# PV of all units in plain float32 on 64 columns a head, and a third raw tile for each of the mixture's weights

## The chip, the cores and the metric

The kernel runs on one core of a Trainium2 chip. The metric is the device time of one execution in microseconds (us). Engines in the profile: PE is TensorE (PEld its weight loads), DVE is VectorE, ACT is ScalarE, POOL is GpSimd, SP issues DMA transfers.

## The reference

Inputs are q, k and v of shape (4, 8, 576, 64): 4 batches, 8 heads, 576 positions, 64 elements a head. Everything is float32.

```
scores = (q @ k.T) / 8; position i sees position j where i // 64 >= j // 64, others get -1e9
attn   = softmax of scores over the last axis (maximum taken off, 1e-9 added to the sum)
x      = attn @ v, heads side by side: 2304 tokens x 512
p      = domain_probs / (sum over the 4 experts + 1e-9)
out    = sum over e of p[:, e] * (relu(x @ w1[e]) @ w2[e])   # w1[e] 512 x 1024, w2[e] 1024 x 512
```

## The kernel before, in words

**Two precisions.** A float32 product is made in one of two ways. Split: both operands are cut into a high part and a low part in float32r (a cast, then a subtraction), and the products of the parts are added up in PSUM. Plain: TensorE multiplies float32 as it is.

**The mixture** works on five blocks of tokens (BLOCKS): a first one of 256 (the first 64 positions of the four batches) and four of 512 (positions 64 to 575 of one batch each). A block has 32 chunks (4 experts, 8 slices of 128 hidden units). A chunk is mm1 (12 matmuls of the split form, L1035), the relu split into hh and hl, and mm2 (per 128 tokens 3 matmuls, L1080) into four accumulators. For each chunk, 256 KB of w1 and of w2 are loaded to a raw tile (w1r, w2r, two of each), cast to w1h or w2h and subtracted to w1l or w2l (four of each). A raw tile comes free when its subtraction is done.

**The attention.** The first block's attention is done at the start by itself. The rest is 16 units: one pair of heads of one batch, 512 queries against 576 keys. The scores are kept transposed, keys on partitions, queries on columns, in five pieces of 512, 448, 320, 192 and 64 columns (pieces_of); C = 1536 is their sum. The last piece, of 64 keys, has both heads on one half of the partitions each. Units of batch 0 (plain, ph == 1) run during the mixture's first block; the four units of batch b run during the mixture's block of batch b - 1. The code spreads a unit over threads: k_thread, q_thread, v_thread (loads and splits), s_thread (scores into two PSUM banks, att), e_thread (out of PSUM into the tile S, and a running maximum in cm), m_thread (maximum over keys by GpSimd, subtraction, exponential), pv_flow (product with V, normalization, and x split into xh and xl).

**What differs by unit before the change.** In the four plain units, by_piece subtracts and exponentiates piece by piece over both heads, sum_up adds the pieces into sa, and pv_flow makes, in one stretch on TensorE, the product with V in float32 with each head's 64 columns on its own half of the PSUM partitions (L777), and then the sums over keys by a matmul with ones. V comes straight into a tile VN, whose middle 64 columns hold ones. In the twelve other units, exp_head takes the exponential of a whole head (L715), casts 1472 columns to PH and subtracts to PL; V is loaded to vr and split into VS; for each head the product is a chain of nine steps in one bank: four pieces of PH against [Vh, Vl], the 64-column piece in plain float32 against VJ, four pieces of PL (L809). The bank's two halves are then added (a copy to rc and an addition to xs). The sums are added in place in S and reduced over partitions by GpSimd (L733).

**What sets the order.** Flow is a planner that runs when the program is built: each thread yields operations, with the engine or engines that may do it, a cost in ns, what it reads and the buffers it uses. The planner keeps a clock for each engine and emits the operation that can start first by its estimate (ties by priority). A thread that wants a buffer (take) waits until one is given back. So each engine's queue has one order written down beforehand, and an engine stands where the next instruction's inputs are late, whatever else is ready behind. `late` tells the planner to assume a further delay (LAG / 2 = 750 ns for the product with V).

Of the kernel before, what the change touches and what calls it, by code (L numbers as in the profile page):

```python
# [9 lines left out]
F32R = mybir.dt.float32r  # L10
# [7 lines left out]
PEO = 13.5  # L18


NARROW = 64
# [185 lines left out]
def kernel(  # L207
# [50 lines left out]
    wide_of = [[x[2] for x in pieces_of(j[1], j[2])[0] if x[2] > NARROW] for j in every]  # L258
    MAXE = max(sum(x) for x in wide_of)
    MAXT = max(len(x) for x in wide_of)  # L260
# [12 lines left out]
    bufs("w1r", 2, [P, KC, P])  # L273
    bufs("w2r", 2, [P, DM])
# [7 lines left out]
    bufs("vr", 1, [P, MAXT, 2, D])  # L282
# [5 lines left out]
    bufs("VS", 2, [P, MAXT, 4, D], F32R)  # L288
    bufs("VJ", 2, [P, 2, 3, D])
# [4 lines left out]
    bufs("PL", 2, [P, MAXE], F32R)  # L294
    bufs("PH", 2, [P, MAXE], F32R)
    bufs("cm", 1, [P, 2 * MAXW])
    bufs("mx", 1, [P, 2 * MAXW])
    bufs("sa", 1, [P, 2 * MAXW])
    bufs("xs", 1, [P, MAXW])
# [27 lines left out]
    def late(o, by):  # L327


        o.lag = by  # L330
        return o
# [52 lines left out]
    def unit(u, ua, us, ju, pu, ph, job, dst, c):  # L384
# [5 lines left out]
        wide, narrow = [x for x in pcs if x[2] > NARROW and not plain], [x for x in pcs if x[2] <= NARROW or plain]  # L390
        ce = sum(x[2] for x in wide)
# [67 lines left out]
        def v_thread():  # L459
            yield ("until", lambda: now[0] >= gate[u])  # L460
            vals, jv, got = [], [], []
            n = len(wide)
            VS = None
            VJ = yield (fl.take("VN", u) if plain else fl.take("VJ", us))
            if n:
                vr = yield fl.take("vr", us)
                VS = yield fl.take("VS", us)
                for h in range(2):
                    vals.append((yield dma(vr.tile[:, :n, h, :], v[b, h0 + h, :P * n].rearrange("(t p) d -> p t d", p=P),
                                           n * P * 256, u=[vr], prio=pr + 0.005)))  # L470
            keep = sorted(j for j, *_ in narrow if j is not None)
            for h in range(2):
                if plain:
                    jv.append((yield dma(VJ.tile[:, VJ.tile.shape[1] - 1, 2 * h, :], v[b, h0 + h, q1 - P:q1], P * 256,
                                         u=[VJ], prio=pr + 0.005)))
                elif odd:
                    jv.append((yield dma(VJ.tile[64 * h:64 * h + 64, VJ.tile.shape[1] - 1, 1, :], v[b, h0 + h, q1 - MASK_BLOCK:q1], 64 * 256,
                                         u=[VJ], prio=pr + 0.005)))
                if keep:
                    jv.append((yield dma(VJ.tile[:, :len(keep), 2 * h, :],  # L480
                                         v[b, h0 + h, P * keep[0]:P * keep[-1] + P].rearrange("(t p) d -> p t d", p=P),
                                         len(keep) * P * 256, u=[VJ], prio=pr + 0.005)))
            if n:
                vs = VS.tile[:, :n]
                a = yield a_copy(vs[:, :, 0:4:3, :], vr.tile[:, :n], n * 128, vals, [vr, VS], pr + 0.005)
                l = yield tt(BOTH, vs[:, :, 1:3, :], vr.tile[:, :n], vs[:, :, 0:4:3, :], SUB, n * 128, [a], [vr, VS],
                             pr + 0.005)
                got += [a, l]
                fl.give(vr)
            st["v"] = (VS, VJ, got, jv)  # L490

# [163 lines left out]
        def by_piece(Sb, Sv, mx, mv, m):  # L655
# [8 lines left out]
            def sum_up():  # L664
# [3 lines left out]
                for i, (_, a, w, c0) in enumerate(todo[1:]):  # L668
                    yield ("until", lambda: len(exps) > i + 1)
                    r = a - q0  # L670
                    if i == 0:
                        got.append((yield a_copy(av[:, :, :r], Sv[:, :, :r], 2 * r, exps[:1], [Sb, sa], pr)))
                    t = yield tt("dve", av[:, :, r:], av[:, :, r:] if i else Sv[:, :, r:W], Sv[:, :, c0:c0 + w], ADD, 2 * w,
                                 exps[i:i + 2] + got[1:], [Sb, sa], pr)
                    got = got[:1] + [t]
                for h in range(2):
                    st["P"][h] = (None, None, None, None, Sb, exps)
                st["sums"] = (sa, got)
# [8 lines left out]
        def m_thread():  # L687
# [13 lines left out]
            st["P"] = {}  # L701
            st["exp"] = []

            if plain:
                yield from by_piece(Sb, Sv, mx, mv, m)
                return
            subs = []
            for _, a, w, c0 in pcs:
                sv, mb = Sv[:, :, c0:c0 + w], mv[:, :, a - q0:W]
                subs.append((yield tt("dve", sv, sv, mb, SUB, 2 * w, [m] + st["evac"], [Sb, mx], pr)))  # L710
            fl.give(mx)

            def exp_head(h):
                PH = PL = a = l = None
                j = yield op("act", 0.833 * C + 95, lambda _: nc.scalar.activation(  # L715
                    Sv[:, h, :C], Sv[:, h, :C], AF.Exp, scale=scale), subs, [Sb], pr)
                if wide:
                    PH = yield fl.take("PH", pu + h)
                    PL = yield fl.take("PL", pu + h)
                    a = yield a_copy(PH.tile[:, :ce], Sv[:, h, :ce], ce, [j], [Sb, PH], pr)  # L720
                    l = yield tt("dve", PL.tile[:, :ce], Sv[:, h, :ce], PH.tile[:, :ce], SUB, ce, [j, a], [Sb, PH, PL], pr)
                st["P"][h] = (PH, PL, a, l, Sb, j)

            for h in range(2):
                yield from exp_head(h)

            got = [x for h in range(2) for x in st["P"][h][2:4] + st["P"][h][5:]]
            for _, a, w, c0 in pcs[1:]:
                acc = Sv[:, :, a - q0:W]
                got = [(yield tt("dve", acc, acc, Sv[:, :, c0:c0 + w], ADD, 2 * w, got, [Sb], pr))]  # L730
            st["sums"] = []
            for h in range(2):
                st["sums"].append((yield op("pool", 150 + 6.3 * W, lambda _, h=h: nc.gpsimd.partition_all_reduce(  # L733
                    Sv[:, h, W:2 * W], Sv[:, h, :W], P, RED.add), got, [Sb], pr)))
# [3 lines left out]
        fl.spawn(pv_flow(st, q0, dst, c, W, wide, narrow, C, plain, pr, bank_tag))  # L738
# [13 lines left out]

    def pv_flow(st, q0, dst, c, W, wide, narrow, C, plain, pr, bank_tag):
        yield ("until", lambda: "v" in st)
        VS, VJ, vv, jv = st["v"]
        xs = yield fl.take("xs")
        rc = yield fl.take("rc", st["ua"])
        parts, sums = [], []
        if plain:
            yield ("until", lambda: "sums" in st)  # L760
            sa, sv = st["sums"]
            PJ, pj = st["P"][1][4:]
            two = []
            for _ in range(2):
                two.append((yield fl.take("att", None, bank_tag)))

            def fn(_):

                for x, todo in zip(two, (narrow, [(None, None, W, 0)])):
                    for i, (j, _a, w, c0) in enumerate(todo):  # L770
                        for g in range(2):
                            if x is two[0]:
                                lhsT = VJ.tile[:, VJ.tile.shape[1] - 1 if j is None else j, 2 * g, :]
                                rhs = PJ.tile[:, g * C + c0:g * C + c0 + w]
                            else:
                                lhsT, rhs = VJ.tile[:, 0, 1, :], sa.tile[:, g * W:g * W + W]
                            nc.tensor.matmul(out=x.tile[64 * g:64 * g + 64, W - w:W], lhsT=lhsT, rhs=rhs,  # L777
                                             start=(i == 0), stop=(i == len(todo) - 1))

            m = yield op("pe", 450.0 + (C + W) / 0.6, fn, jv + pj + sv, [*two, VJ, PJ, sa], pr)  # L780
# [8 lines left out]
            sums.append((yield op([("act", 0.833 * W + 55), ("dve", 1.04 * W + 70)], 0, fn, [m], [two[1], rc], pr)))  # L789
            parts.append((yield a_copy(xs.tile[:, :W], two[0].tile[:, :W], W, [m], [two[0], xs], pr, True)))  # L790
            fl.give(*two)
        for h in range(0 if plain else 2):
            yield ("until", lambda: h in st.get("P", ()))
            PH, PL, a, l, PJ, pj = st["P"][h]
            pb = yield fl.take("att", None, bank_tag)
            ps = pb.tile
            todo = []
            for x, split, dep in ((PH, True, a), (PJ, False, pj), (PL, True, l)):
                for j, _a, w, c0 in wide if split else narrow:
                    if split:  # L800
                        lhsT, cost, dv, c1 = VS.tile[:, j, 2 * h:2 * h + 2, :], w / 2.4 + PEO, vv, c0
                    else:
# [410 lines left out]
```

## Time and profile before

| | us |
|---|---|
| median of 3 runs (lowest, highest) | 931.5 (931.19, 933.13) |
| the profiled execution | 932.45 |
| its span | 930.7 |
| PE, DVE, ACT, POOL busy | 915.3, 728.9, 438.2, 138.7 |
| granted TensorE clock | 0.999 |

The span is the time from the first to the last instruction in the trace. Matmuls are pipelined: the duration of one, as it is shown, overlaps the next, so the distance from start to start is what a matmul takes of TensorE's time.

### The profile page before, as it was taken

Reading aid. Unit: us, or ns where it says so; the run is one execution under the profiler, and the core shown is the slowest. Engines: PE = TensorE matmul, PEld = TensorE weight load, DVE = VectorE, ACT = ScalarE, POOL = GpSimd, SP = SyncE. Lnnn points to the kernel's source line nnn. Section 1 sums busy time; section 2 is a strip of 40 time slices with the busy share of each in tenths; the row PEclk is TensorE's granted clock in tenths of the full one; section 3 lists DMA queues with packets and bytes.
Section 4 is the critical chain, followed back from the end, with each engine's and each line's share of the span. In section 5 each row is a group of like instructions: output and inputs, shape, how many; then the busy total and the mean of one; then the engine's idle time right before and its main releaser. Section 6 shows DMA issues by size and latency. Waiting matters only on the chain.

```text
span 930.7 us, 12721 instructions
## 1 busy us (share of the span) xinstructions
PE 915.3 (98%) x4398; PEld 750.8 (81%) x4398; DVE 728.9 (78%) x1291; ACT 438.2 (47%) x774; POOL 138.7 (15%) x57
## 2 busy tenths in 40 slices
PE   8999999999999999999999999999999999999998
PEld 4677788888887888887888888888888888888886
DVE  7789999989897888878988888888988754445442
ACT  3577765655463454454454545464534322322220
POOL 1111101222103201212131202012121200000000
PEclk9999999999999999999999999999999999999999
DMA  9755466534532445351623545343423343333321
GB/s 166 181 163 165 136 154 189 116 115 93 145 85 80 113 140 137 108 135 46 149 72 100 128 121 154 104 105 113 116 90 90 92 148 102 92 100 94 100 57 45
DMA packets 236162, 107.97 MB, mean 116 GB/s; under 512 B 131393, under 2 KB 213313, under 8 KB 236097
## 3 DMA queue, kind: packets, MB, share of 16 engines
q1 hardware_dynamic: 232928, 106.38, 42.8%
q10 hardware_dynamic: 3168, 0.79, 0.5%
q8 instruction: 34, 0.56, 0.2%
q14 instruction: 32, 0.25, 0.1%
HBM read 102.40 MB, written 4.72 MB: 115 GB/s over the span
## 4 chain that ended last, share of the span: by engine, by line
PE 90%; DVE 4%; DMA 3%; ACT 1%; issue 1%; SPq 1%; DVEq 0%; ACTq 0%
PE acc L1080 40%; PE h L1035 40%; PE att L809 4%; PE att L539 2%; PE att L540 2%; DMA w1r<-in_moe_w_dram 1%; SPq L334 1%; PE acc L777 1%; PE att L777 1%; DVE w2l L347 1%; DMA S<-in_v_dram 1%; DVE cm L347 1%; PE att L527 1%; DVE w1l L347 0%; DMA w2r<-in_moe_w_dram 0%
## 5 line engine op out<-in xcount | busy, mean ns | idle before, releaser
L1035 PE MATMUL h<-xh,w1h 128*128 128x512 f32 (+1 forms) x640 | 237.9, 372 | 0.0
L1035 PE MATMUL h<-xh,w1l 128*128 128x512 f32 (+1 forms) x640 | 236.1, 369 | 1.6 <-DVE w1l L347 1.6
L1035 PE MATMUL h<-xl,w1h 128*128 128x512 f32 (+1 forms) x640 | 235.6, 368 | 0.1
L1080 PE MATMUL acc<-w2h,hh 128*128 128x512 f32 x576 | 227.0, 394 | 0.0
L1080 PE MATMUL acc<-w2h,hl 128*128 128x512 f32 x576 | 224.7, 390 | 1.0 <-DVE hl L1054 1.0
L1080 PE MATMUL acc<-w2l,hh 128*128 128x512 f32 x576 | 224.6, 390 | 0.0
L1052 ACT ACTIVATE hh<-h 128x512 fp32r<-128x512 f32 (+1 forms) x160 | 88.9, 556 | 184.6 <-PE h L1035 183.5
L347 DVE TENSOR_TENSOR w2l<-w2r,w2h 128x512 fp32r<-128x512 f32 x160 | 112.9, 706 | 56.2 <-ACT w2h L340 55.8
L340 ACT CAST w2h<-w2r 128x512 fp32r<-128x512 f32 x148 | 92.2, 623 | 136.1 <-PE acc L1080 132.0
L1035 PEld LDWEIGHTS h<-xh,w1l 128*128 128x128 f32 x640 | 120.4, 188 | 22.7 <-DVE w1l L347 2.4
L1035 PEld LDWEIGHTS h<-xh,w1h 128*128 128x128 f32 x640 | 120.5, 188 | 21.0 <-issue 1.2
L1035 PEld LDWEIGHTS h<-xl,w1h 128*128 128x128 f32 x640 | 120.6, 188 | 19.8 <-DVE xl L347 0.3
L1054 DVE SCALAR_TENSOR_TENSOR hl<-h,hh 128x512 fp32r<-128x512 f32 (+1 forms) x160 | 100.6, 629 | 35.9 <-ACT hh L1052 35.4
L1080 PEld LDWEIGHTS acc<-w2h,hl 128*128 128x128 f32 x576 | 108.1, 188 | 25.0 <-DVE hl L1054 1.9
L1080 PEld LDWEIGHTS acc<-w2h,hh 128*128 128x128 f32 x576 | 108.3, 188 | 23.9 <-issue 2.5
L347 DVE TENSOR_TENSOR w1l<-w1r,w1h 128x512 fp32r<-128x512 f32 x160 | 119.3, 745 | 8.2 <-ACT w1h L340 4.4
L1080 PEld LDWEIGHTS acc<-w2l,hh 128*128 128x128 f32 x576 | 108.3, 188 | 20.0
L733 POOL PARTITION_ALL_REDUCE S<-S x24 | 79.8, 3374 | 242.4 <-DVE S L347 223.9
L696 POOL PARTITION_ALL_REDUCE mx<-cm x16 | 54.4, 3398 | 355.8 <-DVE cm L347 270.3
L340 ACT COPY S<-att 128x512 f32<-128x512 f32 (+2 forms) x90 | 48.7, 542 | 71.3 <-DVE att L609 48.6
L340 ACT CAST w1h<-w1r 128x512 fp32r<-128x512 f32 x116 | 71.6, 619 | 19.4 <-DMA w1r<-in_moe_w_dram 19.1
L347 DVE TENSOR_TENSOR S<-S,mx 128x1024 f32<-128x1024 f32 (+4 forms) x80 | 60.0, 790 | 5.4 <-POOL mx L696 5.4
(135 smaller groups left out, 862.3 us busy)
## 6 DMA issues: line engine op xcount, KB each, us to landing
w1r<-in_moe_w_dram SPq DMA_DIRECT2D x160, 256.0 KB, 2.8
w2r<-in_moe_w_dram SPq DMA_DIRECT2D x160, 256.0 KB, 2.8
qr<-in_q_dram SPq DMA_DIRECT2D x112, 64.0 KB, 2.3
kr<-in_k_dram SPq DMA_DIRECT2D x64, 72.0 KB, 2.8
out_dram<-o SPq DMA_DIRECT2D x16, 256.0 KB, 2.3
vr<-in_v_dram SPq DMA_DIRECT2D x24, 128.0 KB, 2.6
VN<-in_v_dram SPq DMA_DIRECT2D x8, 128.0 KB, 3.1
S<-in_k_dram SPq DMA_DIRECT2D x4, 128.0 KB, 4.7
```

The costliest lines, as they stand in the source:

```text
L340: o = op(engs, 0, lambda e: nc.scalar.copy(dst, src) if e == "act" else nc.vector.tensor_copy(dst, src), r, u, prio)
L347: o = op(engs, 0, lambda e: ENG[e].tensor_tensor(out=dst, in0=a, in1=b, op=alu), r, u, prio)
L539: nc.tensor.matmul(out=o, lhsT=KK.tile[:, at:at + n], rhs=Hv[:, hs, lo:W], start=True, stop=False)
L540: nc.tensor.matmul(out=o, lhsT=KK.tile[:, at:at + n], rhs=Lv[:, hs, lo:W], start=False, stop=True)
L696: lambda _: nc.gpsimd.partition_all_reduce(mx.tile[:, :2 * W], src, P, RED.max),
L733: st["sums"].append((yield op("pool", 150 + 6.3 * W, lambda _, h=h: nc.gpsimd.partition_all_reduce(Sv[:, h, W:2 * W], Sv[:, h, :W], P, RED ...
L777: nc.tensor.matmul(out=x.tile[64 * g:64 * g + 64, W - w:W], lhsT=lhsT, rhs=rhs, start=(i == 0), stop=(i == len(todo) - 1))
L809: nc.tensor.matmul(out=o, lhsT=lhsT, rhs=rhs, start=(i == 0), stop=(i == n - 1))
L1035: nc.tensor.matmul(out=ps[:, :n], lhsT=s.tile[:, ks], rhs=x.tile[:, kc, :n], start=(kc == 0 and m == 0), stop=(kc == KC - 1 and m == 2),)
L1052: a = yield op("act", 0.833 * n + 55, lambda _: nc.scalar.activation(hh.tile[:, :n], ps[:, :n], AF.Relu), [mm], [pb, hh], 0.0)
L1054: l = yield op("dve", 1.04 * n + 70, lambda _: nc.vector.scalar_tensor_tensor(out=hl.tile[:, :n], in0=ps[:, :n], scalar=0.0, in1=hh.tile[: ...
L1080: nc.tensor.matmul(out=acc, lhsT=s.tile[:, ts], rhs=w.tile, start=(f == 0 and m == 0), stop=(f == FC - 1 and m == 2))
```

## The change

Every unit takes its exponentials by by_piece and its product with V in plain float32, with each head's 64 columns on its own half of the partitions. PH, PL, VS, vr and VJ go, with their casts and subtractions; V comes straight into VN. In the twelve units the sums stay with GpSimd, but are added in sa and reduced into a new tile sb. The room is used for a third w1r and a third w2r.

```diff
-    bufs("w1r", 2, [P, KC, P])
-    bufs("w2r", 2, [P, DM])
+    bufs("w1r", 3, [P, KC, P])
+    bufs("w2r", 3, [P, DM])
-    bufs("vr", 1, [P, MAXT, 2, D])
-    bufs("VS", 2, [P, MAXT, 4, D], F32R)
-    bufs("VJ", 2, [P, 2, 3, D])
-    bufs("PL", 2, [P, MAXE], F32R)
-    bufs("PH", 2, [P, MAXE], F32R)
+    bufs("sb", 1, [P, 2 * MAXW])
...
         def v_thread():
+            VJ = yield fl.take("VN", u)
+            at = VJ.tile.shape[1] - 1
             for h in range(2):
+                r, o, n = (slice(0, P), 2 * h, P) if plain else (slice(64 * h, 64 * h + 64), 1, MASK_BLOCK)
+                jv.append((yield dma(VJ.tile[r, at, o, :], v[b, h0 + h, q1 - n:q1], n * 256, u=[VJ], prio=pr + 0.005)))
+                jv.append((yield dma(VJ.tile[:, :nt, 2 * h, :], v[b, h0 + h, :P * nt].rearrange("(t p) d -> p t d", p=P),
+                                     nt * P * 256, u=[VJ], prio=pr + 0.005)))
+            st["v"] = (VJ, jv)
...
             def sum_up():
...
-                for h in range(2):
-                    st["P"][h] = (None, None, None, None, Sb, exps)
-                st["sums"] = (sa, got)
+                st["P"] = (Sb, exps)
+                if plain:
+                    st["sums"] = (sa, got)
+                    return
+                sb = yield fl.take("sb", us)
+                sums = []
+                for h in range(2):
+                    sums.append((yield op("pool", 150 + 6.3 * W, lambda _, h=h: nc.gpsimd.partition_all_reduce(
+                        sb.tile[:, h * W:h * W + W], sa.tile[:, h * W:h * W + W], P, RED.add), got, [sa, sb], pr)))
+                fl.give(sa)
+                st["sums"] = (sb, sums)
...
-            if plain:
-                yield from by_piece(Sb, Sv, mx, mv, m)
-                return
...
+            yield from by_piece(Sb, Sv, mx, mv, m)
...
     def pv_flow(...):
+        yield ("until", lambda: ("sums" if plain else "P") in st)
+        PJ, pj = st["P"]
+        sa, sv = st["sums"] if plain else (None, [])
+        two = []
+        for _ in range(2 if plain else 1):
+            two.append((yield fl.take("att", None, bank_tag)))
+        def fn(_):
+            for x, todo in zip(two, (pcs, [(None, None, W, 0)])):
+                for i, (j, _a, w, c0) in enumerate(todo):
+                    for g in range(2):
+                        if x is two[0]:
+                            lhsT = VJ.tile[:, j, 2 * g, :] if j is not None else VJ.tile[:, nj, 2 * g if plain else 1, :]
+                            rhs = PJ.tile[:, g * C + c0:g * C + c0 + w]
+                        else:
+                            lhsT, rhs = VJ.tile[:, 0, 1, :], sa.tile[:, g * W:g * W + W]
+                        nc.tensor.matmul(out=x.tile[64 * g:64 * g + 64, W - w:W], lhsT=lhsT, rhs=rhs,
+                                         start=(i == 0), stop=(i == len(todo) - 1))
+        m = yield late(op("pe", 450.0 + (C + (W if plain else 0)) / 0.6, fn, jv + pj + sv,
+                          [*two, VJ, PJ] + ([sa] if plain else []), pr), 0.0 if plain else LAG / 2)
+        fl.give(VJ, PJ)
...
+        part = yield a_copy(xs.tile[:, :W], two[0].tile[:, :W], W, [m], [two[0], xs], pr, True)
+        fl.give(*two)
...
-                n = b.tile.shape[1] - 1
-                nc.gpsimd.memset(b.tile[:, :n, 1, :], 0.0)
-                nc.gpsimd.memset(b.tile[:, n, 0:3:2, :], 0.0)
+        for b in fl.free["VN"]:
+            nc.gpsimd.memset(b.tile[:, :, 1, :], 1.0)
```

## Rows read from the trace of the kernel before

**Rows 1.** The page, its first part: busy time, share of the span, instructions.

```profile
PE 915.3 (98%) x4398; PEld 750.8 (81%) x4398; DVE 728.9 (78%) x1291; ACT 438.2 (47%) x774; POOL 138.7 (15%) x57
```

**Rows 2.** Stretches: length; busy us (instructions) of PE, PEld, DVE, ACT, POOL; clock, DMA, GB/s.

```profile
137.00:336.00 199.00, 197.21 (x923) 164.59 (x922) 176.04 (x305) 109.60 (x180) 40.67 (x12) 1.00 0.46 118
...
540.00:750.00 210.00, 210.00 (x967) 175.68 (x967) 177.40 (x311) 98.66 (x160) 39.94 (x12) 1.00 0.41 111
```

**Rows 3.** The chain that ended last, at 154 us: start us, us, what.

```profile
154.76 2.72 PE h L1035 x12
```

**Rows 4.** Waits of TensorE, 23 to 137 us: total us, times, longest us.

```profile
PE h L1035 <- DVE w1l L347: 1.2, 2, 0.8
PE acc L1080 <- DVE hl L1054: 1.0, 1, 1.0
PE att L527 <- ACT cm L340: 0.7, 1, 0.7
```

**Rows 5.** Waits of TensorE, 137 to 750 us.

```profile
PE att L539 <- DVE cm L347: 2.8, 4, 1.1
PE h L1035 <- DVE w1l L347: 0.4, 1, 0.4
PE att L540 <- DVE LL L347: 0.3, 1, 0.3
```

**Rows 6.** Order of time on TensorE, 172 to 182 us: start, length, instruction, records.

```profile
172.28 0.84 PE L809 MATMUL att<-PH,VS 128*128 128x512 f32 x4
172.96 0.35 PE L809 MATMUL att<-S,VJ 128*128 128x64 f32 x2
173.12 0.47 PE L1035 MATMUL h<-xh,w1h 128*128 128x512 f32 x1
173.44 0.39 PE L1035 MATMUL h<-xl,w1h 128*128 128x512 f32 x1
...
174.59 0.83 PE L809 MATMUL att<-PL,VS 128*128 128x512 f32 x4
...
175.51 0.39 PE L1080 MATMUL acc<-w2l,hh 128*128 128x512 f32 x1
...
180.08 0.84 PE L809 MATMUL att<-PH,VS 128*128 128x512 f32 x4
...
181.93 0.40 PE L1035 MATMUL h<-xl,w1h 128*128 128x512 f32 x1
```

**Rows 7.** Order of time on TensorE around a plain unit's product, 132 to 137 us.

```profile
132.47 0.28 PE L1035 MATMUL h<-xh,w1l 128*128 128x256 f32 x1
132.68 2.81 PE L777 MATMUL att<-S,VN 128*64 128x512 f32 x20
135.32 1.03 PE L777 MATMUL acc<-sa,VN 128*64 128x512 f32 x4
136.28 0.50 PE L1080 MATMUL acc<-w2h,hh 128*128 128x512 f32 x1
136.61 0.39 PE L1080 MATMUL acc<-w2l,hh 128*128 128x512 f32 x1
```

**Rows 8.** Groups on VectorE, 137 to 750 us: busy us, mean ns, idle before.

```profile
L347 DVE TENSOR_TENSOR PL<-S,PH 128x1472 fp32r<-128x1472 f32 x24 | 40.3, 1682 | 0.2
...
L347 DVE TENSOR_TENSOR xs<-att,rc 64x512 f32<-64x512 f32 x24 | 16.4, 685 | 1.1 <-ACT rc L340 0.8
...
L340 DVE CAST PH<-S 128x1472 fp32r<-128x1472 f32 x11 | 10.1, 919 | 0.1
```

**Rows 9.** Groups on ScalarE, whole span.

```profile
L340 ACT CAST PH<-S 128x1472 fp32r<-128x1472 f32 x13 | 18.6, 1430 | 0.3
```

**Rows 10.** Waits of SP's queue, 140 to 930 us.

```profile
SPq L334 <- DVE w1l L347: 267.3, 97, 10.9
```

**Rows 11.** Order of time on SP and ScalarE, 27 to 31 us.

```profile
27.30 0.53 SPq L334 DMA_DIRECT2D w1r<-in_moe_w_dram  x1
...
30.31 0.62 ACT L340 CAST w1h<-w1r 128x512 fp32r<-128x512 f32 x1 [2.10 <-DMA w1r<-in_moe_w_dram]
```

More of the change, by code (lines that the diff above doesn't have):

```diff
@@ L18 @@
 PEO = 13.5
-NARROW = 64
 BLOCKS = [[(b, 0, MASK_BLOCK) for b in range(4)]] + [[(b, MASK_BLOCK, 576)] for b in range(4)]
@@ L257 @@
     MAXC = max(pieces_of(j[1], j[2])[1] for j in every)
-    wide_of = [[x[2] for x in pieces_of(j[1], j[2])[0] if x[2] > NARROW] for j in every]
-    MAXE = max(sum(x) for x in wide_of)
-    MAXT = max(len(x) for x in wide_of)
     fl = Flow()
@@ L389, in unit @@
         pcs, C = pieces_beside(q0, q1) if plain else pieces_of(q0, q1)
-        wide, narrow = [x for x in pcs if x[2] > NARROW and not plain], [x for x in pcs if x[2] <= NARROW or plain]
-        ce = sum(x[2] for x in wide)
         h0 = 2 * c
@@ L460, in v_thread @@
             yield ("until", lambda: now[0] >= gate[u])
[L461 to L467, printed above, removed]
-                for h in range(2):
-                    vals.append((yield dma(vr.tile[:, :n, h, :], v[b, h0 + h, :P * n].rearrange("(t p) d -> p t d", p=P),
-                                           n * P * 256, u=[vr], prio=pr + 0.005)))
@@ L471, in v_thread @@
-            keep = sorted(j for j, *_ in narrow if j is not None)
-            for h in range(2):
-                if plain:
[L474 to L490, printed above, removed]
+            jv = []
+            VJ = yield fl.take("VN", u)
+            at = VJ.tile.shape[1] - 1
@@ L700, in m_thread @@
             mv = mx.tile[:, :2 * W].rearrange("p (h w) -> p h w", h=2)
-            st["P"] = {}
-            st["exp"] = []
-            if plain:
-                yield from by_piece(Sb, Sv, mx, mv, m)
-                return
[L707 to L734, printed above, removed]
+            yield from by_piece(Sb, Sv, mx, mv, m)
         for t in (k_thread, q_thread, v_thread, s_thread, e_thread, m_thread):
             fl.spawn(t())
-        fl.spawn(pv_flow(st, q0, dst, c, W, wide, narrow, C, plain, pr, bank_tag))
+        fl.spawn(pv_flow(st, q0, dst, c, W, pcs, C, plain, pr, bank_tag))
     def x_take(bi):
@@ L748, in x_take, with pv_flow @@
         yield ("until", lambda: X[bi] is not None)
-    def pv_flow(st, q0, dst, c, W, wide, narrow, C, plain, pr, bank_tag):
+    def pv_flow(st, q0, dst, c, W, pcs, C, plain, pr, bank_tag):
         yield ("until", lambda: "v" in st)
-        VS, VJ, vv, jv = st["v"]
+        VJ, jv = st["v"]
+        nj = VJ.tile.shape[1] - 1
         xs = yield fl.take("xs")
         rc = yield fl.take("rc", st["ua"])
-        parts, sums = [], []
-        if plain:
[L760 to L780, printed above, removed]
@@ L787, in fn @@
                     nc.vector.tensor_scalar_add(rc.tile[:, :W], ps[:, :W], 1e-9)
[L789 to L802, printed above, removed]
-                        nj = VJ.tile.shape[1] - 1
-                        lhsT = VJ.tile[:, nj, 1 - h:3 - h, :]
-                        cost, dv, c1 = 2 * max(107.0, 2 * w / 2.4 + 2.5), jv, h * C + c0
-                    todo.append((lhsT, x.tile[:, c1:c1 + w], w, cost, dv + [dep]))
-            for i, (lhsT, rhs, w, cost, dep) in enumerate(todo):
-                def fn(_, o=ps[:, W - w:W], lhsT=lhsT.rearrange("p g d -> p (g d)"), rhs=rhs, i=i, n=len(todo)):
-                    nc.tensor.matmul(out=o, lhsT=lhsT, rhs=rhs, start=(i == 0), stop=(i == n - 1))
-                m = yield late(op("pe", max(107.0, cost), fn, dep, [pb] + [x for x in (VS, VJ, PH, PL, PJ) if x], pr), LAG / 2)
-            hi, lo = slice(64 * h, 64 * h + 64), slice(64 - 64 * h, 128 - 64 * h)
-            fl.give(PH, PL)
-            x = yield a_copy(rc.tile[hi, :W], ps[lo, :W], W, [m], [pb, rc], pr, True)
-            parts.append((yield tt("dve", xs.tile[hi, :W], ps[hi, :W], rc.tile[hi, :W], ADD, W, [m, x], [pb, rc, xs], pr)))
-            fl.give(pb)
-        fl.give(VJ, PJ) if plain else fl.give(VS, VJ)
+            sums = yield op([("act", 0.833 * W + 55), ("dve", 1.04 * W + 70)], 0, fn, [m], [two[1], rc], pr)
+        part = yield a_copy(xs.tile[:, :W], two[0].tile[:, :W], W, [m], [two[0], xs], pr, True)
+        fl.give(*two)
         rt, n = rc.tile, W // 32
@@ L824, in pv_flow @@
         if plain:
-            got = yield op("dve", 1.04 * W + 70, lambda _: nc.vector.transpose(out=t1, in_=rt[:, :W]), sums, [rc, tr], pr)
+            got = yield op("dve", 1.04 * W + 70, lambda _: nc.vector.transpose(out=t1, in_=rt[:, :W]), [sums], [rc, tr], pr)
         else:
-            yield ("until", lambda: len(st.get("sums", ())) == 2)
-            for h, s in enumerate(st["sums"]):
+            yield ("until", lambda: "sums" in st)
+            sb, sums = st["sums"]
+            for h, s in enumerate(sums):
                 hi = slice(64 * h, 64 * h + 64)
                 got = yield op("dve", 1.04 * W + 70, lambda _, h=h, hi=hi: nc.vector.transpose(
-                    out=t1[hi], in_=PJ.tile[hi, h * C + W:h * C + 2 * W]), [s], [PJ, tr], pr)
-            fl.give(PJ)
+                    out=t1[hi], in_=sb.tile[hi, h * W:h * W + W]), [s], [sb, tr], pr)
+            fl.give(sb)
             got = yield op("dve", 80.0, lambda _: nc.vector.tensor_scalar_add(t2, t0, 1e-9), [got], [tr, tc_], pr)
@@ L838, in pv_flow @@
         fl.give(tr, tc_)
-        d = yield tt("dve", xs.tile[:, :W], xs.tile[:, :W], rt[:, :W], MUL, W, parts + got, [xs, rc], pr)
+        d = yield tt("dve", xs.tile[:, :W], xs.tile[:, :W], rt[:, :W], MUL, W, [part] + got, [xs, rc], pr)
         fl.give(rc)
@@ L1175 @@
                 nc.gpsimd.memset(t[64 * h:64 * h + 64, :, 64 - 64 * h:128 - 64 * h], 0.0)
-        for tag in ("VN", "VJ"):
-            for b in fl.free[tag]:
-                if tag == "VN":
-                    nc.gpsimd.memset(b.tile[:, :, 1, :], 1.0)
-                    continue
-                n = b.tile.shape[1] - 1
-                nc.gpsimd.memset(b.tile[:, :n, 1, :], 0.0)
-                nc.gpsimd.memset(b.tile[:, n, 0:3:2, :], 0.0)
+        for b in fl.free["VN"]:
+            nc.gpsimd.memset(b.tile[:, :, 1, :], 1.0)
         fl.run()
```

## The prediction

> **What bounds the kernel now.** I read the page first: TensorE is busy 98% of the span, VectorE 78%, ScalarE 47%, GpSimd 15% [rows 1]. A share of 98% can hide stages with other limits, so I cut the span into stretches next. In the mixture's second block (137 to 336 us) TensorE is busy 197.21 of 199 us with VectorE at 176.04; in the fourth (540 to 750) it is busy 210.00 of 210 [rows 2]. The chain of waits says what fills it: twelve mixture matmuls of 512 columns take 2.72 us, 0.227 us each, one behind the other [rows 3]. The waits of TensorE's queue come third: from 23 us to the end of the first block it loses 1.2 + 1.0 + 0.7 = 2.9 us [rows 4], from 137 to 750 us 2.8 + 0.4 + 0.3 = 3.5 us, nearly all of it for VectorE [rows 5]. So TensorE's instructions, in order, set the end. An edit pays in two ways only: it takes columns or switches off TensorE, or it lets VectorE answer in time where TensorE now stands. Weight transfers have no row of their own among these waits.
>
> **The product with V, before.** Twelve units (one pair of heads of one of the batches 1 to 3) run the split form. In the last view, the order of time, I measure from start to start and subtract the mixture's 0.227 us. Head 0: the four pieces of PH and the 64-column plain piece begin at 172.28, the second mixture matmul behind them at 173.44: 1.16 - 0.23 = 0.93 us. The four pieces of PL begin at 174.59 and the matmul behind begins at 175.51, which makes 0.92 - 0.23 = 0.69 us. Head 1, with nothing between its parts: 180.08 to 181.93, less 0.23, is 1.62 us [rows 6]. Together 3.24 us a unit. The mixture's matmul behind a plain piece starts its successor late (173.12 to 173.44 is 0.32 us, not 0.23), and that surcharge is in the sum.
>
> **The product with V, after.** The trace has this form already, in the four units of batch 0: two heads side by side in 64 columns each, pieces of 512, 448, 320, 192 and 64 columns, which are the widths that the twelve units have. The ten matmuls show as 20 records from 132.68 to 135.32: 2.64 us for 1536 columns a head, 1.72 ns a column for both heads at once. Around them: the last mixture matmul before holds until 132.68, 0.21 us after 132.47, where its kind (256 columns, 12 in a row) has a pace of 0.12, so 0.09 us on entry. The block of sums behind has 512 columns, 512 x 1.72 ns = 0.88 us, and lasts 135.32 to 136.28, 0.96 us: 0.08 us of tail. The first mixture matmul behind takes 0.33 us (136.28 to 136.61) in place of 0.23: 0.10 us [rows 7]. In the twelve units no sums follow (GpSimd makes them as before), so the tail and the 0.10 fall to the product itself: 2.64 + 0.09 + 0.08 + 0.10 = 2.91 us. The saving is 0.33 us a unit, 12 x 0.33 = 4.0 us. Bounds: if the switches in and out cost nothing, 3.24 - 2.64 = 0.60 us, 7.2 us in all; if each side costs double, 0.06 us, 0.7 us in all. I take 4.0, since the four shown units are the same instructions.
>
> Here a page speaks against the change. Rows 7 and 6 show two heads side by side at 1.72 ns a column, where the plain 64-column piece of one head over the whole array took 173.12 - 172.96 = 0.16 us, 2.5 ns a column. The Trainium skill (TensorE: Matmul & The Clock Gate, "Measured speedup vs the span model") puts three column tiles at 2.38 times the speed of one, 0.79 of the ideal. An estimate by that page's ratio, two tiles at 1.59 times, gives 5.28 / 1.59 = 3.3 us for the body and no gain at all. The trace disagrees, and it is this kernel's own form.
>
> **VectorE and ScalarE.** What goes from VectorE between 137 and 750 us: 24 subtractions for PL, 40.3 us; 11 casts to PH, 10.1; 24 additions of the two halves out of PSUM, 16.4 [rows 8]. That is 66.8 us, a little over a tenth of 613 us, and the V splits go too. From ScalarE go 13 casts to PH, 18.6 us [rows 9], and 24 copies out of PSUM; it gains one copy of the result a unit, a small copy for the sums, and five exponentials where there were two. At 47% ScalarE hides this; if that cover were gone the delay would fall on the unit's product (the second rival). The additions for the sums, GpSimd's reductions and the transposes stay. SP issues as many V transfers a unit as before, four, of the same bytes.
>
> What is this worth to TensorE? Its waits of 3.5 us in [rows 5] are for banks of scores that VectorE frees late, and 2.9 us in [rows 4] are for splits and hidden activations behind a full VectorE queue. Bounds: all 6.4 us go, or the new order written by the planner adds as much again (the planner fills the time that it believes free, so relief is not kept as slack in full). I take a third of 6.4, 2.1 us: nearer to no gain, because the scores' side, where the largest waits are, is not edited.
>
> **Third raw tiles.** In the steady state SP stands 267.3 us for w1l alone, that is for a raw tile to come free [rows 10], and TensorE loses nothing by it; a third tile turns this wait into an earlier transfer: 0 us, covered by four split tiles of each kind ahead of TensorE. At the start it may matter: the fourth w1 tile is only issued at 27.30, and ScalarE idles 2.10 us for it before the cast at 30.31 [rows 11]. With a third tile each weight transfer may be issued one release sooner. Against it: K and Q of the second unit, which are behind it in SP's queue, then come later. Both feed the waits of [rows 4], so their worth is inside the 2.1 us.
>
> **Sum.** 4.0 + 2.1 = 6.1 us off the profiled execution of 932.45 us (span 930.7 and 1.75 around it): 926.35. The profiled execution lies 0.95 above the median of the runs, 931.5; taken off that, 925.4 us.
>
> **Rivals.**
> Relief in full: all of the 6.4 us of waits go. For it: from 540 to 750 us TensorE already has none. Against: the waits of the first block come with units that aren't edited. 931.5 - 4.0 - 6.4 = 921.1.
> Gain spent on new waits: the planner's new order meets VectorE late elsewhere, 3 us more than now (about the 3.5 us of [rows 5] once more). 931.5 - 4.0 + 3 = 930.5.
> Slower, the fused product comes late: before, a unit's product was four groups, each waiting for its own tile; now one block of 2.6 us waits for five exponentials of both heads, and the mixture's matmuls behind it in TensorE's queue wait too. Price: the waits for the scores average 2.8 / 4 = 0.7 us; at 0.7 us in each unit, 8.4 us, 931.5 - 4.0 + 8.4 = 935.9. It decides from 0.33 us a unit with no relief. Against it: no product with V, split or plain, has a row among the waits.
> Heads not side by side in the new units: the body is 2 x 2.64, 12 x 2.64 = 31.7 us more than forecast for the product, 931.5 - 4.0 + 31.7 = 959. Partial overlap, as the page's ratio has it, would cost 12 x (3.3 - 2.64) = 8 us more, 933.4 with the 2.1 us kept. Against both: [rows 7].
>
> **Chances.** Forecast (922.5 to 928.5) 0.50; relief in full 0.15; gain spent 0.19; late product 0.12; heads not or only partly side by side 0.04. A measurement here tells about 0.2%, 1.9 us. Faster than 929.6: the first two and a third of the third, 0.71. Within 0.2%: the rest of the third, 0.13. Slower: the last two, 0.16. Range: from 919.0, a little under relief in full, to 932.5, which leaves out the late product and part of the spent gain.
>
> **What would show it.** The twelve units' product must show as 20 records in about 2.64 us with no wait ahead; a wait of TensorE for an exponential of ScalarE there is the late product. VectorE's busy time must fall by 60 to 80 us (less where weight casts move to it), and the waits of [rows 4] and [rows 5] must shrink to about two thirds. The mixture's twelve must stay at 2.72 us. The prediction is wrong if the span falls without TensorE's product being shorter, or if the waits together grow beyond 10 us.

## The result and the profile after

| | before | after |
|---|---|---|
| median, us (lowest to highest, 4 runs each) | 932.26 (931.19 to 933.13) | 921.13 (920.6 to 922.43) |
| profiled execution, span | 932.45, 930.7 | 920.6, 918.8 |
| PE, DVE, ACT busy | 915.3, 728.9, 438.2 | 909.7, 665.5, 404.5 |

The ratio is 0.9883, 95% interval 0.9866 to 0.9901: 11 us faster, where 6.1 were forecast. The time lies in the stated range, but outside the forecast's own band of 922.5 to 928.5: it is what the first rival (relief in full, 921.1) gave.

The product with V, in the order of time on TensorE in the changed kernel (start, length, records), answers to [rows 6]:

```profile
174.65 0.39 PE L953 MATMUL h<-xh,w1l 128*128 128x512 f32 x1
174.96 2.81 PE L718 MATMUL att<-S,VN 128*64 128x512 f32 x20
177.70 0.50 PE L953 MATMUL h<-xh,w1h 128*128 128x512 f32 x1
178.04 0.39 PE L953 MATMUL h<-xl,w1h 128*128 128x512 f32 x1
```

From 174.65 to 178.04 are 3.39 us; two mixture matmuls of 0.227 taken off, 2.94 us a unit (forecast 2.91, before 3.25). All twelve units show these figures: measured in this way they take 35.3 us, where those of the kernel before take 39.0. Nothing waits ahead of any of them, and the mixture's twelve still take 2.72 us.

The waits of TensorE in the changed kernel, whole span, answer to [rows 4] and [rows 5]; the four left out lie before 22 us:

```profile
PE h L953 <- DVE xl L337: 1.5, 1, 1.5
...
PE att L506 <- DVE cm L337: 0.3, 1, 0.3
```

Of 6.4 us 1.8 are left, and the 1.5 is a wait that the kernel before did not have. From 137 us to the last block TensorE is busy 602.72 of 603 us (before 599.45), with VectorE and ScalarE freer (length; PE, PEld, DVE, ACT, POOL busy; before, then after):

```profile
137.00:740.00 603.00, 599.45 (x2773) 500.25 (x2772) 522.05 (x903) 306.06 (x501) 120.76 (x36) 1.00 0.43 113
```

```profile
137.00:740.00 603.00, 602.72 (x2807) 487.00 (x2804) 464.97 (x854) 274.74 (x499) 121.94 (x36) 1.00 0.44 115
```

A view that I had not read before predicting shows where else to look: ScalarE's waits from 23 to 137 us. First the kernel before (waited for: us, times, longest):

```profile
ACT hh L1052 <- PE h L1035: 13.0, 14, 1.4
ACT w1h L340 <- DMA w1r<-in_moe_w_dram: 12.4, 9, 2.8
```

and the changed kernel:

```profile
ACT hh L970 <- PE h L953: 12.6, 15, 2.2
...
ACT w2h L330 <- DMA w2r<-in_moe_w_dram: 1.3, 2, 1.0
```

For w1's transfer ScalarE stood 12.4 us in the first block; that row is gone. The first mixture chunk of 512 columns (the 33rd chunk, where the second block begins) starts at 149.74 us before and at 144.79 after. Not all of this is the block's own work: of the scores of the units that come next, 12 matmuls (2.6 us) stand ahead of that chunk before and 4 (0.9 us) after, so 1.7 of the 4.95 us are work that moved behind it.

### The profile page after: what moved, and what is told of

It reads as the page before. It is cut to its first block, busy times and chain, and to the rows that moved or that the text cites. A ratio compares the mean times of both kernels' runs of the same rounds, so it can differ in the third digit from the quotient of the medians.

```text
span 918.8 us, 12715 instructions
## 1 busy us (share of the span) xinstructions
PE 909.7 (99%) x4398; PEld 732.0 (80%) x4398; DVE 665.5 (72%) x1237; ACT 404.5 (44%) x768; POOL 139.2 (15%) x53
## 4 chain that ended last, share of the span: by engine, by line
PE 93%; DVE 3%; DMA 2%; SPq 1%; issue 0%; POOL 0%; ACT 0%; DVEq 0%; POOLq 0%
PE h L953 42%; PE acc L998 41%; PE att L718 4%; PE att L507 2%; PE att L506 2%; SPq L324 1%; PE att L494 1%; PE acc L718 1%; DMA S<-in_v_dram 1%; DVE o L1034 1%; PE acc L494 0%; DVE hl L972 0%; POOL sb L651 0%; DVE S L337 0%; DMA kr<-in_k_dram 0%
## 5 line engine op out<-in xcount | busy, mean ns | idle before, releaser
L337 DVE TENSOR_TENSOR w2l<-w2r,w2h 128x512 fp32r<-128x512 f32 x160 | 109.3, 683 | 74.8 <-ACT w2h L330 74.1
L337 DVE TENSOR_TENSOR w1l<-w1r,w1h 128x512 fp32r<-128x512 f32 x160 | 112.7, 705 | 5.5 <-PE acc L998 0.5
L651 POOL PARTITION_ALL_REDUCE sb<-sa x24 | 80.4, 3397 | 129.9 <-DVE sa L337 118.9
L330 DVE CAST w1h<-w1r 128x512 fp32r<-128x512 f32 x71 | 31.8, 447 | 47.8 <-PE h L953 44.1
```

Of the source, the lines that this page charges most:

```text
L330: o = op(engs, 0, lambda e: nc.scalar.copy(dst, src) if e == "act" else nc.vector.tensor_copy(dst, src), r, u, prio)
L337: o = op(engs, 0, lambda e: ENG[e].tensor_tensor(out=dst, in0=a, in1=b, op=alu), r, u, prio)
L651: sums.append((yield op("pool", 150 + 6.3 * W, lambda _, h=h: nc.gpsimd.partition_all_reduce(sb.tile[:, h * W:h * W + W], sa.tile[:, h * W ...
```

## The experiments

All compare with the kernel before on the same chip. Medians in us, ratios with 95% intervals. The chips differ (the median of the kernel before is 932.3 to 934.0 us), so the ratios are what can be compared between rows.

| run | median | ratio | 33rd chunk begins |
|---|---|---|---|
| changed kernel | 921.13 | 0.9883 (0.9866 to 0.9901) | 144.79 |
| two raw tiles (e1) | 926.99 | 0.9926 (0.9909 to 0.9943) | 150.43 |
| dead split (e2) | 924.42 | 0.9903 (0.9886 to 0.9919) | 145.88 |
| second bank held (e3) | 922.31 | 0.9884 (0.9867 to 0.9902) | 146.29 |
| before, third raw tiles (e4) | 927.81 | 0.9941 (0.9926 to 0.9956) | 145.57 |
| third tile for w1 alone (e5) | 922.17 | 0.9889 (0.9873 to 0.9906) | 146.83 |
| third tile for w2 alone (e6) | 928.86 | 0.9956 (0.9941 to 0.9971) | 154.99 |
| four raw tiles (e7) | 922.2 | 0.9886 (0.9871 to 0.9901) | 144.14 |
| splits held back (e8) | 925.34 | 0.9913 (0.9895 to 0.993) | 148.54 |
| heads one after the other (e9) | 947.71 | 1.0152 (1.0135 to 1.017) | 147.11 |
| third chunk's splits held back (e10) | 924.67 | 0.9907 (0.9892 to 0.9922) | 148.23 |
| changed, allowance 140 (e11) | 922.85 | 0.9888 (0.9871 to 0.9904) | 145.04 |
| before, allowance 140 (e12) | 934.68 | 1.0011 (0.9996 to 1.0026) | 154.77 |

**The new product alone (e1).**

```diff
-    bufs("w1r", 3, [P, KC, P])
-    bufs("w2r", 3, [P, DM])
+    bufs("w1r", 2, [P, KC, P])
+    bufs("w2r", 2, [P, DM])
```

> The changed kernel with two raw tiles of each weight again, so the new product with V alone. Measured: 921.1 us after, 932.3 before; TensorE's product gives 12 x (3.25 - 2.94) = 3.7 us of the 11.1, about 7 to 8 us come from waits that went. Theory (relief of VectorE and ScalarE ends the waits): the third tiles matter at the start only, 921 to 923.5 us, chunk 32 of the mixture within 2 us of the changed kernel's. Rival (third raw tiles end the waits of the first block): 925 to 927 us, with the first block as long as before (chunk 32 begins near 149.7 us, where the changed kernel has 144.8).

0.9926 against 0.9883: the third tiles are worth 0.43%, 4.0 us, and it lies ahead of the 33rd chunk. From that chunk to the end the kernel with two tiles is no slower (923.1 - 150.43 = 772.7 us; with three 918.8 - 144.79 = 774.0; before 930.7 - 149.74 = 781.0). The rival on the first block holds. The chunk's delay of 5.6 us overstates it: in this execution the first mixture matmul begins at 23.79 us, against 22.23 in the changed kernel (e9 and e10, with three tiles, begin as late, at 24.13 and 24.23), and six more matmuls of the next units' scores, 1.0 us, stand ahead of the chunk. Without both, the first block (first mixture matmul to 33rd chunk, scores left out) takes 124.8 us with two tiles, 121.7 with three, and 124.5 in the kernel before: 3.1 us by the traces. ScalarE's waits there are those of before:

```profile
ACT w1h L330 <- DMA w1r<-in_moe_w_dram: 11.5, 8, 3.0
```

TensorE's own waits name the weight too (whole span):

```profile
PE h L953 <- DVE w1l L337: 1.7, 4, 0.8
PE h L953 <- ACT w1h L330: 0.9, 1, 0.9
```

Waits for w1h or w1l stand in the traces of all four kernels with two raw tiles for w1 (before 1.6 us, e1 2.6, e6 5.1, e12 2.2) and in none of the ten with three or four.

**Vector work without the new product's relief (e2).** Added ahead of the product with V in the twelve units:

```diff
+    bufs("PL", 2, [P, 1472], F32R)
+    bufs("PH", 2, [P, 1472], F32R)
...
-                st["P"] = (Sb, exps)
...
+                for h in range(2):
+                    PH = yield fl.take("PH", pu + h)
+                    PL = yield fl.take("PL", pu + h)
+                    hi = yield a_copy(PH.tile, Sv[:, h, :1472], 1472, exps, [Sb, PH], pr)
+                    yield tt("dve", PL.tile, Sv[:, h, :1472], PH.tile, SUB, 1472, exps + [hi], [Sb, PH, PL], pr)
+                    fl.give(PH, PL)
+                st["P"] = (Sb, exps)
```

> The changed kernel, with the casts to PH and the subtractions to PL of the twelve units put back as work whose result nobody reads, ahead of the product with V in the order of planning. TensorE's instructions are those of the changed kernel. Theory (relief): VectorE is as busy as before between 137 and 750 us (some 50 us more) and most of the waits there come back: 924 to 928 us. Rival (the waits went with the PSUM banks, one instead of two a unit, or with the third raw tiles): 920.5 to 922.5 us.

0.9903 against 0.9883 is 0.20%, 1.9 us. The two intervals overlap, and 1.9 us above the changed kernel's 921.1 is 923.0, between the two expected ranges: the time alone does not decide. From the 33rd chunk to the end of the span it takes 922.5 - 145.88 = 776.6 us, the changed kernel 774.0; e3, e7, e8, e10 and e11, which have none of the dead work, take 774.0 to 776.0. The profiles agree with the theory in kind: part of the waits comes back, 1.6 us, by other names, with VectorE at 514 us. Busy time as above, then TensorE's waits from 137 to 750 us:

```profile
137.00:740.00 603.00, 601.48 (x2799) 483.80 (x2796) 514.01 (x865) 309.76 (x536) 143.18 (x36) 1.00 0.44 114
```

```profile
PE att L509 <- DVE LL L339: 1.2, 3, 0.7
PE att L508 <- DVE cm L339: 0.4, 2, 0.2
```

The dead work is not the old work in every respect: a subtraction for PL takes 2136 ns here (1682 in [rows 8]).

**A second PSUM bank held (e3).**

```diff
+        spare = [] if plain else [(yield fl.take("att", None, bank_tag))]
...
-        fl.give(*two)
+        fl.give(*two, *spare)
```

> The changed kernel, in which each of the twelve units' products holds a second PSUM bank of the scores' two, unused, until the result is copied out. Rival (banks): the next unit's scores wait again, 923 to 926 us, with waits of the scores' matmuls for VectorE or ScalarE of 2 to 4 us in all. Theory (relief): 920.5 to 922.5 us, waits under 1 us as in the changed kernel.

Ratio 0.9884, TensorE's wait for the scores' banks unchanged from 137 us on: banks are not the cause.

```profile
PE att L506 <- DVE cm L337: 0.3, 1, 0.3
```

**Third raw tiles in the kernel before (e4).**

```diff
-    bufs("w1r", 2, [P, KC, P])
-    bufs("w2r", 2, [P, DM])
+    bufs("w1r", 3, [P, KC, P])
+    bufs("w2r", 3, [P, DM])
...
-    bufs("VS", 2, [P, MAXT, 4, D], F32R)
+    bufs("VS", 1, [P, MAXT, 4, D], F32R)
```

> The kernel before with a third raw tile of each weight; for the room, one tile VS in place of two. Theory (relief): the start gains up to 2 us, the rest stays: 930 to 933 us. Rival (third raw tiles end the first block's waits): 926 to 928 us, chunk 32 of the mixture beginning near 145 us.

0.9941, 5.5 us: the third tiles pay without the new product. The theory, which gave them 2 us, falls. The 33rd chunk begins 4.2 us earlier, but 1.7 of that are scores that moved behind it; counted as in e1, the first block takes 122.5 us in place of 124.5. Some 2.5 us came behind it, where e1 shows no worth of the third tiles; whether that is the tiles, the VS tile less or the order is open. ScalarE's wait for w1 is shorter, not gone (23 to 137 us):

```profile
ACT w1h L340 <- DMA w1r<-in_moe_w_dram: 7.0, 6, 2.6
```

So the length of this wait is no price: it is 7.0 us here, 9.5 in e8 and 6.2 in e11, and in none of the three does TensorE wait for w1.

**Which kind (e5, e6), and one more (e7).** One bufs line changed in each of the first two, both to 4 in the third.

> The changed kernel with a third raw tile for w1 alone (w2r two). With both third tiles chunk 32 of the mixture began at 144.8 us, with neither at 150.4 and the time was about 4 us longer. Theory (w1's transfer is the one that comes late: ScalarE stood 2.1 us for the fourth w1 tile at 30.3, TensorE's waits of the first block name w1l): 920.5 to 922.5 us, chunk 32 within 1 us of 144.8. Rival (both kinds are needed, since mm1 and mm2 of each chunk of 2.8 us want one each): 923 to 925.5 us.

> The changed kernel with a third raw tile for w2 alone (w1r two). Theory (w1's transfer is the late one): as without third tiles, 924.5 to 927 us, chunk 32 near 150 us, TensorE's waits for w1l back. Rival (both kinds): 923 to 925.5 us.

> The changed kernel with four raw tiles of each weight. Theory (the first block lost time since a raw tile came back too late for transfer, cast and subtraction; with three, VectorE and ScalarE set the pace): within 1.5 us of the changed kernel, 920 to 922.5 us. Rival (the first block is still held by transfers): 917 to 919.5 us, chunk 32 near 142 us.

w1's tile alone gives nearly all (0.9889; its 33rd chunk begins 2.0 us late, not within the 1 us expected). w2's alone gives nothing or less (0.9956, with neither 0.9926; slower than either range). With w2's alone TensorE's largest wait is for w1l again, six times in the first block, and ScalarE's is what it was (TensorE 23 to 160 us, ScalarE 23 to 137):

```profile
PE h L953 <- DVE w1l L337: 4.2, 6, 0.9
```

```profile
ACT w1h L330 <- DMA w1r<-in_moe_w_dram: 11.5, 9, 3.8
```

A fourth tile changes nothing: with three, a later return of raw tiles no longer sets the first block's pace.

**The start's order (e8, e10).** In e8 for i >= 1, in e10 for i >= 2:

```diff
     def w_split(which, i, raw, src, v0, pr):
+        if i >= 1:
+            yield ("until", lambda: left_first[0] == 0)
         hi = yield fl.take(f"w{which}h", i)
```

> The changed kernel, in which the splits of the second and later chunks' weights are planned only after the first block's x is split. In the changed kernel TensorE waits 1.5 us at 23.6 for xl, behind splits of later chunks on VectorE, and its clock is granted at 0.62 to 0.81 for some 4 us behind that, 1.1 us more. Theory (the new tiles brought these splits ahead of xl): both go, 917.5 to 919.5 us. Rival (the delayed splits are late for chunk 1 and the time comes back as waits for w1l): 920.5 to 923 us.

> The changed kernel, with the wait for the first block's x on the splits of the third and later chunks' weights alone. Theory (the wait for xl at 23.6 us comes from the third chunk's split on VectorE ahead of it, which the third raw tiles allow; the second chunk's is needed early): that wait falls below 0.6 us, the clock stays granted, 918 to 920 us. Rival (any shift of the start's order is paid back by the order behind it): 920.5 to 926 us.

Both theories miss; the time of e8 lies above its rival's range too, that of e10 within its rival's. In e8 the wait for xl is gone, but others take its place (TensorE, 23 to 60 us):

```profile
PE att L494 <- DVE qT L434: 1.1, 1, 1.1
PE acc L494 <- DVE qT L434: 0.4, 1, 0.4
PE acc L1000 <- DVE hl L974: 0.2, 1, 0.2
```

and in e10 the wait for xl stays at 1.1 us, with a new one of 2.4 us for the scores:

```profile
PE att L494 <- ACT cm L330: 2.4, 1, 2.4
PE h L955 <- DVE xl L337: 1.1, 1, 1.1
```

No version that I ran beats the changed kernel.

**Heads one after the other (e9).** The loop `for i: for g:` becomes `for g: for i:` in the twelve units.

> The changed kernel, in which the twelve units' products run head 0's five pieces and then head 1's, not the two heads by turns; the columns, the operands and the planner's costs stay. Theory (the product costs 2.64 us since two heads of 64 columns run at the same time): the body of 20 records goes to about 2 x 2.64 = 5.3 us, 12 x 2.64 = 32 us more, 950 to 956 us. Rival (the 64-column form is fast by itself, side by side or not): no change, 920 to 923 us.

947.71, below the range that the theory gave, with the product as the whole reason:

```profile
625.95 5.01 PE L720 MATMUL att<-S,VN 128*64 128x512 f32 x20
630.88 0.50 PE L955 MATMUL h<-xh,w1h 128*128 128x512 f32 x1
```

630.88 - 625.95 = 4.93 us where the changed kernel has 177.70 - 174.96 = 2.74: 12 x 2.19 = 26.3 us, of 26.6 between the medians (25.1 by the ratios). It is a little under the 5.3 expected. In this kernel two heads overlap only when their matmuls come by turns. The ratio 4.93 / 2.74 = 1.80 lies above the estimate of 1.59 that I drew from the Trainium skill (TensorE: Matmul & The Clock Gate, "Measured speedup vs the span model"), which scales that page's three tiles of 32 columns to two; the measurement decides against that estimate.

**Another order of the same work (e11, e12).** `SLACK = 140.0` in place of 100.0.

> The changed kernel with the planner's extra allowance for TensorE's inputs at 140 in place of 100 ns: another order of the same instructions. Theory (third raw tiles and relief, whatever the order): within 2 us of the changed kernel, 919 to 923.5 us. Rival (the changed kernel's order is a lucky one): 924 to 930 us.

> The kernel before with the planner's allowance at 140 ns: another order of the same instructions. Theory: within 2 us of the kernel before, 930 to 934.5 us, with ScalarE's waits for the w1 transfer in the first block (12.4 us before) still over 8 us. Rival (the order of before is an unlucky one): 922 to 928 us.

Both orders land by their own kernel: by the ratios they move the time by 0.5 and 1.0 us, within the intervals. The difference between the two kernels is not luck of one order. The ten executions of e12 run from 932.0 to 937.4 us, and the profiled one is the slowest of them, so up to some 2 us of any term below may be noise. In e12 ScalarE still stands for w1's transfer in the first block:

```profile
ACT w1h L340 <- DMA w1r<-in_moe_w_dram: 8.4, 5, 3.1
```

## Why the prediction was right, and where its sizes were off

**The product with V: right.** 4.0 us forecast; the trace gives 12 x (3.25 - 2.94) = 3.7, and the sum over all twelve units says the same. The rows of the plain units priced it to 0.03 us a unit, the switches in and out included, and e9 shows the reason that was given.

**Third raw tiles: mis-sized.** The failed step is the term that put them at 0 us in the steady state and inside the 2.1 us at the start. The sign was in [rows 4]: TensorE's 1.2 us for w1l, which I put down to a full VectorE queue. From 23 to 137 us VectorE is no less busy in the changed kernel than before (before, then after; the third figure behind the length), and the wait for w1l is gone:

```profile
23.00:137.00 114.00, 110.93 (x688) 85.68 (x688) 101.56 (x194) 80.50 (x182) 13.42 (x4) 1.00 0.61 160
```

```profile
23.00:137.00 114.00, 112.52 (x706) 89.28 (x704) 103.09 (x198) 81.49 (x183) 13.18 (x4) 0.99 0.64 165
```

I read the waits of SP, which are long and, by e1, cost nothing in the blocks of 512 columns, and one wait of ScalarE (2.10 us in [rows 11]), and did not ask how often that one recurs: 9 times, 12.4 us, in a block where a chunk's mixture matmuls take 2.8 us. Measured, the third tiles are worth 4.0 us (e1 against the changed kernel) to 5.5 (e4 against before), by w1's tile (e5, e6). The chain, as I read it: SP may issue w1's next transfer when w1l has freed a raw tile; it lands 2.8 us later; ScalarE's cast waits for it, the subtraction waits for the cast, and TensorE's next mm1 waits for w1h or w1l; the hidden activations and copies out of PSUM queue behind that cast as well. How the 4.0 us divide among these is not shown. In the blocks of 512 columns, whose chunks have 5.44 us of mixture matmuls, the same chain has room. That the length of a chunk is the dividing line is argued from these rows, not tried.

**Waits for VectorE and ScalarE from 137 us on: a third forecast, nearly all went.** 3.5 us in [rows 5], 0.3 after. The size was off, and the share of the dropped splits is not settled: e2 brings 1.6 us of waits back and costs 1.9 us by the ratios, whose intervals overlap. e3 excludes banks. A rival stands untested: the change also gives S back with the product, where before it was held until GpSimd had reduced the sums and VectorE had transposed them. Of the fall in busy time VectorE had 63 us (forecast 60 to 80).

**The sum.** By the experiments, 3.7 for the product, 4.0 for third tiles and 1.9 for relief make 9.6 of 11; alone, the new product with its relief gives 6.9 us (e1) and the tiles 5.5 (e4), together 10.9. The two traces close the sum. From start to start over the whole span, the 11.9 us between the spans are 5.6 us of TensorE's waits (10.8 before, 5.2 after), 3.7 of the product, and 2.4 of mixture matmuls that begin closer behind one another than before, which the view of waits does not count. Rivals: the late product did not occur (no wait ahead of any of the twelve), heads run side by side, and relief in full had the right time by luck: it had no term for the tiles. My forecast was 5 us short, as both mis-sized terms erred to the same side.

## What to carry to other kernels

Think of the number of raw tiles as a rate (argued above, not shown): release, issue, landing and cast have to fit within as many chunks as there are tiles, in the stage with the shortest chunk. Here SP's queue stood 267 us, and with two tiles (e1) the blocks of 512 columns were no slower for it; ScalarE's waits for w1 of 6.2 to 9.5 us in e4, e8 and e11 left TensorE without a wait for w1. What named the missing tile were a few waits of TensorE for the halves of w1, 1.6 us in all: ask of each such wait what its own input waited for. When a form of an operation is already in the trace, price it there with what surrounds it.

## What was not expected

Behind the new wait of 1.48 us for xl the granted clock fell: 256-column matmuls came 0.21 us apart, the 1.2 GHz level, where they take 0.12 at 2.4 GHz (two stretches of the changed kernel; the clock is the third figure from the end):

```profile
23.00:26.00 3.00, 1.52 (x10) 1.32 (x9) 2.97 (x6) 0.62 (x1) 0.00 (x0) 0.81 1.07 228
26.00:29.00 3.00, 3.00 (x15) 2.29 (x16) 2.65 (x5) 1.41 (x3) 0.00 (x0) 0.62 0.46 91
```

Eleven matmuls at 0.09 us more make about 1.0 us. It came in e8 too, behind the wait of 1.1 us for qT that ends at 37 us, with TensorE busy throughout:

```profile
38.00:46.00 8.00, 8.00 (x23) 5.18 (x23) 6.04 (x12) 5.86 (x16) 3.52 (x1) 0.58 0.93 228
```

In the profiled execution that is part of why that version lost. Such a wait is not always followed by it: in e11, with a wait of 1.2 us for xl, the clock from 23 to 60 us is 1.00.
